# Decode kernel with attention and an MLP: most of one row set of w2 goes to other partitions, in small transfers of its own

## The chip, the core and the metric

The kernel runs on one core of one Trainium2 chip. The metric is the device time of one execution in microseconds; the time before is the median of five runs. One more execution was taken with the hardware profiler, and all views of the profile below are of that one. Times in them count from the start of its span unless a duration is meant.

## What is computed

One decoding step for two sequences: a layer norm of x, sliding-window attention over a cached K and V, and, in parallel, an MLP with a squared ReLU. Both results are added to x.

```python
B, Sq, D = 2, 1, 576;  Hq, Hkv, Sk, Dh = 32, 16, 8192, 128;  F = 4608
W = min(4096, max(256, Sk // 4))                 # 2048 keys of the window
xn = layernorm(x)
q  = (xn @ wq).reshape(B, Sq, Hq, Dh)            # k, v: the last W rows of the caches, 2 heads of q to one
p  = softmax(q @ k.T * Dh ** -0.5)
a  = (p @ v).reshape(B, Sq, Hq * Dh) @ wo
h  = relu(xn @ w1 + b1) ** 2
return x + a + (h @ w2 + b2)
```

All inputs and the output are bfloat16. Nearly all the data is read once: the windows of K and V (16.8 MB each), wq and wo (4.7 MB each), w1 and w2 (5.3 MB each).

## The kernel before

**Attention.** The window is worked in eight units u = 0 to 7, each four KV heads of one sequence. A unit's K is one load (`load_k`, L106) of 128 partitions with 16 KB each, and so is its V. `step(u)` transposes K in eight groups on TensorE (`transposes`, L264, as float32 pairs) with copies out of PSUM on ScalarE (L270) and VectorE (L272), multiplies by q (`scores`), and computes the softmax (`softmax`). The product with V of unit u - 2 (`pv`, `pv_end`) is interleaved. `pv_all` does the last two units after step 7. The sums of each head end in `ws`.

**MLP.** `mlp_h` multiplies by w1 (L366, PSUM tiles h_ps), squares (L375) into `hrow`, and turns `hrow` by 18 transposes (L380) into two PSUM tiles hp_0 and hp_1, of which eight copies (L384, ScalarE and VectorE in turn) fill `hT_sb`. hp and the scores' tiles share the PSUM tag "sc", which has two buffers. `mlp_h` stands between step 6 and step 7 in the program, and TensorE keeps the program's order (`keep_in_program_order`).

**Output.** One accumulator `out_ps` takes every product: `out_acc` does four matmuls of 144 columns, on four column strips of the array, for one row of weights per partition. First x + b2 (L422), then, after step 7 and `pv_all`, 32 rows of wo (L446), 18 rows of the first half of w2 (L448), and 18 of the second (L451). A ScalarE copy (L456) and a store (L457) end the kernel. An earlier store of the same shape (L455) goes out before them.

**w2 in memory.** w2 has 4608 rows of 576 values (1152 bytes). Row x * 2304 + 18 * p + r lies in half x on partition p as its r-th row. The first half is one load of all 18 rows (`w2a`, L438). The second is cut by rows: nine into `w2b` (L439), and six, two and one into `w2c` (L441, the list `W2P`), so that 9, 6, 2 and 1 rows land one after another.

**Queues.** SP issues all large loads in the program's order; the loads of w2 go out behind wo (L435), at the end of the program's list. ScalarE issues x, b1, b2 and the stores. The eight rows of b1 come in four transfers of two rows (L418). Completion semaphores are taken in turn from eight; a transfer waits before its issue until the one that had its semaphore last has landed.

Of the kernel before, what the change touches and what calls it, by code (L numbers as in the profile page):

```python
# [8 lines left out]
F32 = mybir.dt.float32  # L9
BF16 = mybir.dt.bfloat16  # L10
# [6 lines left out]
def kernel(  # L17
# [14 lines left out]
    nc = tc.nc  # L32
    P = 128
    B, Sq, D = A_x.shape
# [36 lines left out]
    RB = 32 * (NG4 - 1) + 2 * B  # L71
    WR = Hq * Dh // P
    WC = Dh // WR
    FR = L1 // P
    assert HW == 32 * FR and QH * 2 == NC and NC * WC == 32
    W2P = [(9, 15), (15, 17), (17, 18)]
    R9 = 9
    BS = 16
    MB = BS * (B - 1) + 1
    RM = 32 * (NG4 - 1) + MB  # L80
# [3 lines left out]
    const = ctx.enter_context(tc.tile_pool(name="const", bufs=1))  # L84
    kvpool = ctx.enter_context(tc.tile_pool(name="kvpool", bufs=6))
    wbig = ctx.enter_context(tc.tile_pool(name="wbig", bufs=1))
    w2pool = ctx.enter_context(tc.tile_pool(name="w2pool", bufs=1))
# [3 lines left out]
    psum = ctx.enter_context(tc.tile_pool(name="psum", bufs=1, space=bass.MemoryType.PSUM))  # L91

    def matmul(*a, **k):
        tc.keep_in_program_order(nc.tensor.matmul(*a, **k))  # L94

    def transpose(*a, **k):
        tc.keep_in_program_order(nc.tensor.transpose(*a, **k))  # L97
# [21 lines left out]
        nc.sync.dma_start(out=tl[:, 0:n], in_=w.rearrange("r n -> (r n)").rearrange("(p l) -> p l", p=P))  # L119
        return tl  # L120

    const.tile([P, 144], F32, name="pad_0")
    xb_sb = const.tile([B + 1, D], BF16, name="xb_sb")
    x_sb = xb_sb[0:B, :]
    nc.scalar.dma_start(out=x_sb, in_=x2d)
# [23 lines left out]
    ident = const.tile([P, P], BF16, name="ident")  # L149
# [30 lines left out]
    for t0, half, k0, n, pc in ((0, 0, 0, NK, 0), (0, 1, 0, NK, 1), (1, 0, 1, NK - 1, 1), (1, 1, 0, NK - 1, 0)):  # L180
# [11 lines left out]
                          in_=own[:].unsqueeze(2).to_broadcast([P, NC, WC]))  # L192
# [11 lines left out]
                          in_=ident[0:2 * NG4, 0:2 * NG4].rearrange("p (x g) -> p x g", g=NG4).unsqueeze(3)  # L204
# [3 lines left out]
    w2_rows = B_w2.rearrange("(x p r) n -> x p (r n)", x=2, r=FR)  # L208


    w2c_sb = w2pool.tile([P, (FR - R9) * D], BF16, name="w2c")

    out_ps = psum.tile([RM, OQ], F32, tag="out", name="out_ps")
    nc.vector.memset(out_ps[:], 0.0)
# [1 line left out]
    def out_acc(lhsT, rhs, o, start=False, stop=False):  # L216
        for i in range(4):
            matmul(out_ps[32 * i:32 * i + MB, :], lhsT=lhsT, rhs=rhs[:, o * D + i * OQ:o * D + (i + 1) * OQ],
                   start=start, stop=stop, skip_group_check=True, tile_position=(0, 32 * i))
# [38 lines left out]
    def transposes(u, g):  # L258
        k_f = k_tiles[u][:].bitcast(F32)
        kT_ps = psum.tile([P, JG * P], BF16, tag="kT", bufs=3, name=f"kT_ps_{u}_{g}")  # L260
        kT_f = kT_ps[:].bitcast(F32)
        for i in range(JG // 2):
            j = g * JG // 2 + i
            transpose(out=kT_f[:, i * P:(i + 1) * P], in_=k_f[:, j * P:(j + 1) * P], identity=ident_f[:])  # L264
        t, o = divmod(g, TG)
        if o == 0:
            kT_tiles[(u, t)] = ktpool.tile([P, TG * JG * P], BF16, tag="kT_sb", name=f"kT_{u}_{t}")
        kT = kT_tiles[(u, t)][:, o * JG * P:(o + 1) * JG * P]
        if g % 2 == 0:
            nc.scalar.copy(out=kT, in_=kT_ps[:])  # L270
        else:
            nc.vector.tensor_copy(out=kT, in_=kT_ps[:])  # L272

    def scores(u, t):
        tq, b = divmod(u, B)
        if t == 0:
            sc_tiles[u] = psum.tile([P, NJJ * 32], F32, tag="sc", bufs=2, name=f"sc_ps_{u}")
            matmul(sc_tiles[u][:], lhsT=far_h[:], rhs=is_h, start=True, stop=False, skip_group_check=True)
        sc_ps = sc_tiles[u]
        kT = kT_tiles.pop((u, t))[:].rearrange("p (j k c) -> p j k c", k=P, c=2)  # L280
        z = QZ * (1 - t)
        for c in range(2):
            for g in range(4):
                matmul(sc_ps[32 * g:32 * (g + 1), :], lhsT=qz[:, tq, b, c, z:z + SR],
                       rhs=kT[:, :, 32 * g:32 * (g + 1), c], start=False, stop=(t == NT - 1 and c == 1),
                       skip_group_check=True, tile_position=(0, 32 * g))
# [23 lines left out]
    nc.gpsimd.memset(ws[:], 0.0)  # L310
    hT_sb = const.tile([P, 2, FR, MB], BF16, name="hT_sb")
    nc.gpsimd.memset(hT_sb[:], 0.0)

    def pv(u, part, parts):
        n = NJJ // parts
        if part == 0:
            o_tiles[u] = psum.tile([P, NS * Dh], F32, tag="o", name=f"o_ps_{u}")
        v = v_tiles[u][:].rearrange("p (t j s d) -> p j t s d", t=NT, s=2, d=Dh)
        for j in range(part * n, (part + 1) * n):
            g = j % 4  # L320
            matmul(o_tiles[u][32 * g:32 * (g + 1), :], lhsT=pT_tiles[u][:, j, :], rhs=v[:, j], start=(j < 4),
                   stop=(j >= NJJ - 4), skip_group_check=True, tile_position=(0, 32 * g))
        if part == parts - 1:
            pT_tiles.pop(u)

    def pv_end(u):
        tq, b = divmod(u, B)
        o_ps = o_tiles.pop(u)
        o1 = o1_tiles.pop(u)
        for k in range(NS):  # L330
            kw = dict(out=o1[:, 0:Dh], in0=o_ps[:, k * Dh:(k + 1) * Dh])
            if k == 0:
                nc.vector.tensor_scalar(scalar1=in_s[:, 0:1], scalar2=None, op0=ALU.mult, **kw)
            else:
                nc.vector.scalar_tensor_tensor(scalar=in_s[:, k:k + 1], in1=o1[:, 0:Dh], op0=ALU.mult, op1=ALU.add,  # L335
                                               **kw)

        def fin():
            op = psum.tile([P, Dh + 1], F32, tag="op", name=f"op_ps_{u}")
            pp = slice(32 * tq, 32 * (tq + 1))  # L340
            matmul(op[pp, :], lhsT=of_h[:], rhs=o1[:], start=True, stop=True, skip_group_check=True,
                   tile_position=(0, 32 * tq))
            linv = work.tile([P, 1], F32, tag="linv", name=f"linv_{u}")
            nc.vector.reciprocal(out=linv[pp, :], in_=op[pp, Dh:Dh + 1])
            om_t = work.tile([P, Dh], F32, tag="om", name=f"om_{u}")
            om = om_t[pp, :].rearrange("p (q r) -> p q r", r=WR)
            nc.vector.scalar_tensor_tensor(out=om, in0=op[pp, 0:Dh].rearrange("p (q r) -> p q r", r=WR),
                                           scalar=linv[pp, 0:1], op0=ALU.mult, op1=ALU.mult,
                                           in1=own_c[pp, :].unsqueeze(2).to_broadcast([32, WC, WR]))
            with nc.allow_low_precision(reason="sums of one term and zeros"):  # L350
                nc.vector.tensor_reduce(out=ws[pp, :, BS * b], in_=om.rearrange("p q r -> p r q"), axis=AX.X,  # L351
                                        op=ALU.add)

        return fin

    def mlp_h(w1_sb):
# [20 lines left out]
        for a in range(2):  # L377
# [3 lines left out]
            for g in range(NG4):  # L381
# [2 lines left out]
                cp(out=hT_sb[pp, :, a * nr:(a + 1) * nr, 0:MB:BS].rearrange("p x r b -> p r x b"),  # L384
                   in_=hp[pp, :, 32 * g:32 * g + 2 * B].rearrange("p r (x b) -> p r x b", b=B))

    def step(u):
        fin = None
        w = u - 2
        with_pv = w >= 0  # L390
        for g in range(NG):
            transposes(u, g)
            if with_pv and g == 1:
                pv(w, 0, 2)
            if with_pv and g == 2:
                pv(w, 1, 2)
                fin = pv_end(w)
            if g == TG + 1:
                scores(u, 0)
            if g == TG + 2 and fin:  # L400
                fin()
        scores(u, 1)
        softmax(u)
# [10 lines left out]
    softmax(0)  # L414
    load_v(2)
    b1_rows = B_b1.rearrange("(x n) -> x n", n=HW)
    for i0, i1 in ((0, 2), (2, 4), (4, 6), (6, 8)):
        nc.scalar.dma_start(out=b1_sb[i0:i1, :], in_=b1_rows[i0:i1, :])  # L418
    nc.scalar.dma_start(out=xb_sb[B:B + 1, :], in_=B_b2.rearrange("(o n) -> o n", o=1))
    step(1)  # L420
    load_k(4)
    out_acc(sel_b[:], xb_sb, 0, start=True)  # L422
    for u in range(2, NU - 1):
        step(u)
        if u + 1 < NU - 2:
            load_v(u + 1)
        if u == 4:
            w1_sb = issue_flat(B_w1, "w1")
        if u + 3 < NU:
            load_k(u + 3)  # L430
        if u == 5:
            for v in (NU - 2, NU - 1):
                load_v(v)
    mlp_h(w1_sb)
    wo_sb = issue_flat(A_wo, "wo")  # L435
    w2a_sb = w2pool.tile([P, FR * D], BF16, name="w2a")
    w2b_sb = kvpool.tile([P, R9 * D], BF16, tag="kv", name="w2b")
    nc.sync.dma_start(out=w2a_sb[:], in_=w2_rows[0])  # L438
    nc.sync.dma_start(out=w2b_sb[:], in_=w2_rows[1, :, 0:R9 * D])  # L439
    for r0, r1 in W2P:  # L440
        nc.sync.dma_start(out=w2c_sb[:, (r0 - R9) * D:(r1 - R9) * D], in_=w2_rows[1, :, r0 * D:r1 * D])  # L441
    step(NU - 1)
    pv_all(NU - 2)
    pv_all(NU - 1)
    for r in range(WR):
        out_acc(ws[:, r, :], wo_sb, r)  # L446
    for r in range(FR):
        out_acc(hT_sb[:, 0, r, :], w2a_sb, r)  # L448
    for r in range(FR):
        w, o = (w2b_sb, r) if r < R9 else (w2c_sb, r - R9)  # L450
        out_acc(hT_sb[:, 1, r, :], w, o, stop=(r == FR - 1))  # L451

    fin_sb = work.tile([RM, OQ], BF16, tag="fin", name="fin_sb")
    out_v = out2d.rearrange("b (q n) -> q b n", q=4)
# [33 lines left out]
```

## Time and profile before

| | us |
|---|---|
| five runs, median (lowest to highest) | 134.04 (133.92 to 134.12) |
| the profiled execution | 134.12 |
| its span | 132.2 |

The profiled execution's time is 1.9 above its span, the stretch from the first to the last instruction of the trace.

| engine | busy us | share of the span | instructions |
|---|---|---|---|
| TensorE, matmuls | 84.3 | 64% | 949 |
| TensorE, weight loads | 51.8 | 39% | 949 |
| VectorE | 63.2 | 48% | 176 |
| ScalarE | 46.6 | 35% | 67 |
| GpSimd | 4.9 | 4% | 15 |

The DMA engines moved 53.76 MB at a mean of 407 GB/s. The mean granted TensorE clock was 0.815 of full speed; it was 0.50 from 82 to 103.7 and from 113.9 to 124.2, and again from 127.6 on. When the loads at the end were issued on SP, in order: wo at 95.82, w2a at 96.20, w2b at 96.68, the three of w2c between 97.15 and 101.27. The matmuls on wo start at 119.02, on w2a at 122.84, on w2b at 125.99 and on w2c at 128.09.

A row of digits in the profile has 40 equal slices; each digit is the busy share of a slice in tenths. In a row of a timeline or a chain the first two numbers are start and duration. DMA queues are listed with packets, megabytes and share of the time of 16 engines.

The trace also holds a record of each DMA packet (queue, start, duration, bytes), without the engine that moved it. A transfer ends, on each engine that takes part, with a packet of 4 bytes, the completion.

### The profile page before, as it was taken

How to read it: one execution, taken by the hardware profiler on the slowest of the kernel's cores; microseconds unless marked ns; L12 is line 12 of the kernel's file. 1: busy time of each engine (PE TensorE's matmuls, PEld its weight loads, DVE VectorE, ACT ScalarE, POOL GpSimd, SP SyncE). 2: the span in 40 equal slices, each digit the busy share in tenths (PEclk: the TensorE clock that was granted, in tenths of full speed). 3: DMA queues.
4: the chain of work that ended last, by engine and by line, in shares of the span. 5: the costliest groups of instructions: out<-in, count | busy, mean ns of one | idle time of the engine just before them, and what ended most of it. 6: DMA issues, size and time to landing. Idle time of an engine off the chain costs nothing.

```text
span 132.2 us, 2285 instructions
## 1 busy us (share of the span) xinstructions
PE 84.3 (64%) x949; PEld 51.8 (39%) x949; DVE 63.2 (48%) x176; ACT 46.6 (35%) x67; POOL 4.9 (4%) x15
## 2 busy tenths in 40 slices
PE   0079219699689779687696597003919974619651
PEld 0068102268345435353353353002418631209550
DVE  7765300325558757677496576400074477660000
ACT  5717300318846376094373563200015452000000
POOL 5000000010010010100100100100000001000000
PEclk9999975556999999999999999555555899755775
DMA  3999989999999999999999999999999999899960
GB/s 110 421 462 469 424 373 441 406 456 411 436 424 421 451 406 456 406 446 426 441 424 411 446 493 401 406 451 399 426 446 416 493 384 502 382 401 414 417 259 1
DMA packets 3511, 53.76 MB, mean 407 GB/s; under 512 B 419, under 2 KB 558, under 8 KB 814
## 3 DMA queue, kind: packets, MB, share of 16 engines
q1 hardware_dynamic: 3456, 53.61, 95.1%
q8 instruction: 7, 0.11, 0.3%
q10 hardware_dynamic: 46, 0.02, 0.0%
q14 instruction: 2, 0.02, 0.0%
HBM read 53.62 MB, written 0.00 MB: 406 GB/s over the span
## 4 chain that ended last, share of the span: by engine, by line
DMA 77%; PE 17%; SPq 2%; DVE 1%; issue 1%; ACT 0%; ACTq 0%; DVEq 0%
DMA w<-in_B_w_dram 25%; DMA w2c<-in_B_w_dram 23%; DMA k<-in_A_k_cache_dram 15%; DMA wq<-in_A_wq_dram 13%; PE kT_ps L97 6%; PE h_ps L94 3%; PE q_ps L94 3%; PE sc_ps L94 2%; PE out_ps L94 1%; PE qT_ps L97 1%; SPq L106 1%; PE o_ps L94 1%; DVE qrow L238 1%; DVE qz L254 0%; SPq L438 0%
## 5 line engine op out<-in xcount | busy, mean ns | idle before, releaser
L97 PE MATMUL kT_ps<-ident_f,k 128*128 128x128 f32 x256 | 40.2, 305 | 6.1 <-DMA k<-in_A_k_cache_dram 4.1
L97 PEld LDWEIGHTS kT_ps<-ident_f,k 128*128 128x128 f32 x256 | 31.8, 156 | 19.4 <-issue 10.7
L270 ACT COPY kT<-kT_ps 128x1024 bf16<-128x1024 bf16 x32 | 31.9, 1012 | 17.4 <-PE kT_ps L97 17.2
L272 DVE COPY kT<-kT_ps 128x1024 bf16<-128x1024 bf16 x32 | 21.8, 681 | 5.9 <-PE kT_ps L97 5.6
L94 PE MATMUL sc_ps<-kT,qz 128*32 128x512 bf16 x128 | 10.5, 413 | 6.3 <-DVE kT L272 4.7
L302 ACT ACTIVATE p<-sc_ps,bias 128x512 bf16<-128x512 f32 x8 | 5.5, 687 | 21.3 <-DVE gown L298 18.2
L94 PE MATMUL o_ps<-v,pT 128*32 128x512 bf16 x128 | 10.8, 420 | 0.0
L94 PEld LDWEIGHTS <-xnT 128*4 128x4 bf16 x108 | 3.6, 121 | 17.9 <-issue 16.3
L94 PE MATMUL h_ps<-w,xnT 128*4 128x288 bf16 x72 | 4.5, 442 | 8.7 <-DMA w<-in_B_w_dram 8.7
L305 DVE STREAM_TRANSPOSE pT<-p 128x512 bf16<-128x512 bf16 x8 | 5.7, 711 | 6.0 <-ACT p L302 6.0
L335 DVE SCALAR_TENSOR_TENSOR o<-o_ps,in_s,o 128x128 f32<-128x128 f32 x24 | 8.3, 345 | 0.4
L291 DVE TENSOR_REDUCE m<-sc_ps 128x1 f32<-128x512 f32 x8 | 5.5, 692 | 5.4 <-PE sc_ps L94 5.4
L375 DVE TENSOR_TENSOR hrow<-t 100x1152 bf16<-100x1152 f32 x2 | 2.6, 1355 | 10.4 <-ACT t L373 10.4
L94 PE MATMUL q_ps<-wq,xnT 128*4 128x512 bf16 x36 | 4.0, 627 | 5.2 <-DMA wq<-in_A_wq_dram 5.2
L295 POOL PARTITION_ALL_REDUCE gmax<-m x8 | 2.9, 367 | 105.9 <-DVE m L293 105.9
L94 PE MATMUL op_ps<-o,of_h 128*32 128x129 f32 x16 | 3.4, 299 | 4.6 <-DVE o L335 4.6
L94 PEld LDWEIGHTS <-qz 128*32 128x32 bf16 x128 | 2.2, 98 | 10.5 <-DVE kT L272 7.1
L456 ACT CAST fin_sb<-out_ps 113x144 bf16<-113x144 f32 x1 | 0.3, 280 | 17.0 <-PE out_ps L94 17.0
L97 PE MATMUL pro_ps<-ident,xn_sb 2*128 2x2 bf16 x5 | 0.9, 180 | 6.8 <-DVE xn_sb L171 6.5
L238 DVE CAST qrow<-q_ps 100x512 bf16<-100x512 f32 x1 | 0.7, 692 | 8.5 <-PE q_ps L94 8.5
L94 PE MATMUL out_ps<-wo,ws 128*17 128x144 bf16 x128 | 4.0, 325 | 1.2 <-DVE ws L351 1.2
L94 PEld LDWEIGHTS <-hT_sb 128*17 128x17 bf16 x144 | 3.5, 113 | 3.0 <-issue 2.9
(71 smaller groups left out, 58.2 us busy)
## 6 DMA issues: line engine op xcount, KB each, us to landing
k<-in_A_k_cache_dram SPq DMA_DIRECT2D x8, 2048.0 KB, 20.9
v<-in_A_v_cache_dram SPq DMA_DIRECT2D x8, 2048.0 KB, 21.1
w<-in_B_w_dram SPq DMA_DIRECT2D x1, 5184.0 KB
wq<-in_A_wq_dram SPq DMA_DIRECT2D x1, 4608.0 KB, 17.8
wo<-in_A_wo_dram SPq DMA_DIRECT2D x1, 4608.0 KB
w2a<-in_B_w_dram SPq DMA_DIRECT2D x1, 2592.0 KB, 26.6
w2b<-in_B_w_dram SPq DMA_DIRECT2D x1, 1296.0 KB
w2c<-in_B_w_dram SPq DMA_DIRECT2D x1, 864.0 KB
```

Source lines behind the costliest of these rows:

```text
L94: tc.keep_in_program_order(nc.tensor.matmul(*a, **k))
L97: tc.keep_in_program_order(nc.tensor.transpose(*a, **k))
L106: nc.sync.dma_start(out=tl[:], in_=cache[b, tq * TH:(tq + 1) * TH, S0:Sk, :].rearrange("h (c j) d -> c h (j d)", c=CP))
L238: cp(out=qrow[:, k * QW:(k + 1) * QW].rearrange("p (i a d) -> p i a d", a=2, d=Dh), in_=q_ps[0:RB, k * QW // 2:(k + 1) * QW // 2].rearrang ...
L270: nc.scalar.copy(out=kT, in_=kT_ps[:])
L272: nc.vector.tensor_copy(out=kT, in_=kT_ps[:])
L291: nc.vector.tensor_reduce(out=m1[:], in_=sc_ps[:], axis=AX.X, op=ALU.max)
L295: nc.gpsimd.partition_all_reduce(gmax[:], m2[:], channels=P, reduce_op=ReduceOp.max)
L302: nc.scalar.activation(out=p_sb[:], in_=sc_ps[:], func=ACT.Exp, bias=bias[:, 0:1], scale=scale, accum_out=o1[:, Dh:Dh + 1])
L305: nc.vector.transpose(out=pT[:].rearrange("p j r -> p (j r)"), in_=p_sb[:])
L335: nc.vector.scalar_tensor_tensor(scalar=in_s[:, k:k + 1], in1=o1[:, 0:Dh], op0=ALU.mult, op1=ALU.add, **kw)
L375: nc.vector.tensor_tensor(out=h4[:, :, k * HB:(k + 1) * HB], in0=t4, in1=t4, op=ALU.mult)
```

## The change

One row of the second half of w2, the last (r = 17), is loaded in another way; the other 17 are cut as 11, 3, 2 and 1.

Of the 128 partitions' rows r = 17, those of partitions 7, 15, 23 and so on (16 rows) go to the same partitions of a tile `w2y`, in one transfer. The other 112 go to 56 partitions of a tile `w2x`, two rows on each: partition 64 e + 32 i + 8 q + j of w2 (with j from 0 to 6) goes to partition 32 i + 4 j + q, row e. That is four transfers of 28 partitions. They are issued on SP between w2a and w2b.

The rows of h that belong to `w2x` must lie on the same partitions. `mlp_h` gets an addition at its end: ScalarE copies them out of `hrow` (`h_last`), TensorE transposes them (`hx`, a third tile of the tag "sc"), and ScalarE copies them in two pieces into `hx_sb`. The output gets two `out_acc` for `w2x` and one for `w2y`, between those of w2a and w2b: 80 matmuls for the second half instead of 72. Three memsets on GpSimd clear the new tiles, which are not filled everywhere.

The loads of b1 become seven: six of one row and one of two. `pad_0`, a tile that nobody reads, gets smaller by what the new tiles take.

```diff
-    W2P = [(9, 15), (15, 17), (17, 18)]
-    R9 = 9
+    R9 = 11
+    RL = FR - 1
+    W2P = [(R9, 14), (14, 16), (16, RL)]
+    PL = P // 2
+    NJ7 = 7
...
-    const.tile([P, 144], F32, name="pad_0")
+    const.tile([P, 88], F32, name="pad_0")
...
-    w2c_sb = w2pool.tile([P, (FR - R9) * D], BF16, name="w2c")
+    w2c_sb = w2pool.tile([P, (RL - R9) * D], BF16, name="w2c")
+    w2x_sb = w2pool.tile([PL, 2, D], BF16, name="w2x")
+    nc.gpsimd.memset(w2x_sb[:], 0.0)
+    w2y_sb = w2pool.tile([P, D], BF16, name="w2y")
+    nc.gpsimd.memset(w2y_sb[:], 0.0)
...
+    hx_sb = const.tile([PL, 2, MB], BF16, name="hx_sb")
+    nc.gpsimd.memset(hx_sb[:], 0.0)
...
+        hx = psum.tile([PL, P], BF16, tag="sc", bufs=2, name="hx")
+        h_last = const.tile([RB, PL], BF16, name="h_last")
+        nc.scalar.copy(out=h_last[:].rearrange("p (a j q) -> p a q j", a=2, j=8),
+                       in_=hrow[:, RL:PL * FR:FR].rearrange("p (a q j) -> p a q j", a=2, j=8))
+        transpose(out=hx[:, 0:RB], in_=h_last[:], identity=ident[0:RB, 0:RB])
+        for i in range(2):
+            pp = slice(32 * i, 32 * (i + 1))
+            nc.scalar.copy(out=hx_sb[pp, :, 0:MB:BS],
+                           in_=hx[pp, 0:P].rearrange("p (e i x b) -> p i x e b", e=2, i=2, b=B)[:, i, 1])
...
-    for i0, i1 in ((0, 2), (2, 4), (4, 6), (6, 8)):
+    for i0, i1 in ((0, 1), (1, 2), (2, 3), (3, 4), (4, 5), (5, 6), (6, 8)):
         nc.scalar.dma_start(out=b1_sb[i0:i1, :], in_=b1_rows[i0:i1, :])
...
     nc.sync.dma_start(out=w2a_sb[:], in_=w2_rows[0])
+    w2_last = w2_rows[1, :, RL * D:FR * D]
+    w2_move = w2_last.rearrange("(e i q j) n -> e i j q n", e=2, i=2, q=4)
+    for i in range(2):
+        for e in range(2):
+            nc.sync.dma_start(out=w2x_sb[32 * i:32 * i + 4 * NJ7, e, :], in_=w2_move[e, i, 0:NJ7])
+    nc.sync.dma_start(out=w2y_sb[NJ7:P:8, :], in_=w2_last[NJ7:P:8, :])
     nc.sync.dma_start(out=w2b_sb[:], in_=w2_rows[1, :, 0:R9 * D])
...
-    for r in range(FR):
+    for e in range(2):
+        out_acc(hx_sb[:, e, :], w2x_sb[:, e, :], 0)
+    out_acc(hT_sb[:, 1, RL, :], w2y_sb, 0)
+    for r in range(RL):
         w, o = (w2b_sb, r) if r < R9 else (w2c_sb, r - R9)
-        out_acc(hT_sb[:, 1, r, :], w, o, stop=(r == FR - 1))
+        out_acc(hT_sb[:, 1, r, :], w, o, stop=(r == RL - 1))
```

## The prediction

> **What bounds the kernel now.** I read the DMA queues first, then the chain of waits, then the end on TensorE, then the last two microseconds of DMA. All times are microseconds from the span's start.
>
> ```profile
> DMA  3999989999999999999999999999999999899960
> ...
> q1 hardware_dynamic: 3456, 53.61, 95.1%
> q8 instruction: 7, 0.11, 0.3%
> ...
> q14 instruction: 2, 0.02, 0.0%
> ```
>
> The 16 DMA engines are full from slice 2 to slice 37, and q1, the queue of SP's loads, has 95.1% of them. Time is set by when the last bytes of w2 arrive. The q8 and q14 rows are small transfers of program text that share the same engines.
>
> ```profile
> 97.15 30.90 DMA w2c<-in_B_w_dram
> 128.04 0.04 issue
> 128.09 1.36 PE out_ps L94 x34
> 129.44 0.02 issue
> 129.47 0.28 ACT fin_sb L456
> ```
>
> The chain's end is the w2c load, the matmuls on it, one copy, and the store. The instruction records refine it: w2c is three transfers (6, 2 and 1 rows). The first frees the matmuls at 128.09; they then go four per row, 0.12 a row; but the last four start at 129.12 instead of 129.00, just after SP sees the one-row transfer land at 129.09. They end at 129.42. So the end is the landing of the last row, plus 0.33, plus 0.28, plus the store.
>
> ```profile
> DMA  6899138951246544534343333354332100000000
> ...
> q1 hardware_dynamic: 198, 0.32, 38.5%
> ```
>
> This is 126.9 to 129.1 in 40 slices of 0.055. From 127.5 the busy share is 0.3 to 0.5: five to eight of 16 engines work, the rest have finished. The packet records give the completion packet of the one-row transfer on each engine: 126.89, 127.05, 127.07, 127.07, 127.14, 127.15, 127.29, 127.30; then 127.75 and 127.76; then 128.47, 128.61, 128.64, 128.66, 128.67, 128.71. Eight engines are early, two are 0.6 late, six are 1.4 late. Followed from transfer to transfer, each engine keeps its place within a few ns except for single jumps: one engine by 1.41 to 1.48 after each of the six 16 KB q8 packets before the end (at 30.1, 48.5, 67.9, 83.2, 106.6, 123.3), and one by 0.66 and one by 0.84 after the two 8 KB q14 packets. The mean of the 16 is 127.76, so perfect balance could save 0.95.
>
> **The change, part by part.**
>
> *Moved rows.* Before, row 17 of the second half is 8 packets on every engine. After, 112 of its 128 rows go in four transfers of 28, whose outer sizes are 28 and 7, and 16 rows in one transfer of 16. In the records of q10, a two-row load has two completion packets, a one-row load one, a store of 8 pieces in a 4 by 2 pattern four. So I take seven engines for each of the four transfers (4 rows each) and 16 for the fifth (1 row each): seven engines carry 17 of the rows, nine carry 1.
>
> Prices, from the first-finished engine's completions (120.62, 123.71, 125.79, 126.51, 126.89): 9 rows cost 3.093, then 6 cost 2.076, 2 cost 0.721, 1 costs 0.383. A packet is 47 ns for 1152 B and 386 for 10368 B, hence 4.6 ns plus 42.4 per row; a completion is 6 ns. After: 11 rows 8 x 471 = 3.77; 3 rows 8 x 132 = 1.06; 2 and 1 as now; the single row 0.05. Together 5.99 against 6.27. **The nine engines end 0.28 earlier; the seven 16 x 47 + 4 x 6 ns = 0.78 later than those, 0.50 later than now.** If none of the six late engines is among the seven, the last completion goes from 128.71 to 128.43. Of the seven, the early ones then end at 127.4 to 127.7 and one that is 0.6 late at 128.26.
>
> *Which seven.* The stores' packets start 6 ns after the 127.75 and 127.76 completions on two of their four engines and at once on the other two. Those four engines, to which small transfers go (I number them 0 to 3 and suppose that a transfer on seven takes 0 to 6), hold both 0.6-late engines and no 1.4-late one. For 4 to 6 I have only an order. The first late engine started its first k_0 packet among four that began together at 2.75; the other five began at 2.23, 2.33, 2.37, 2.47 and 2.48, in the order in which the text packets hit them (for the fifth the records leave 2.25 possible). Text goes round the engines in turn, it seems, and engines start in blocks. The only run of six consecutive numbers in 4 to 15 whose first has three early fellows in its block of four, and is its last, is 7 to 12. I take it, at about 8 in 10.
>
> The Trainium skill speaks against and for this. "DMA: Bandwidth & Descriptors", section "Why a DMA increments its semaphore by 16 and not by 1", has a transfer use the largest number up to 16 that divides both outer sizes, and the lowest-numbered engines: 7 for 28 and 7. Its "Rules for kernel authors" ask to use all 16 and to coalesce under 64 KB, and these move 32 KB; by its fixed 2.0 us each, five transfers in a row would add 10 and give 144. The trace agrees with the first and not the last: packets of the next transfer start 6 ns after a completion when the queue is full.
>
> *b1.* Four transfers become seven on ACT, six of one row. In the records each b1 packet waits for one wq packet of 1.36 and costs its engine 47 to 51 ns. The first engine gets 3 rows more (+0.15), the second 3 fewer (-0.15); the second is a 0.6-late one, so it ends near 128.1. Both stay below 128.43: 0 on the path. ACT issues them at 4.44 to 5.6 (1.16 for four, so +0.9), with the square root for the norm queued behind; it may also wait, as one semaphore serves every eighth transfer, until an early one lands (8.25 or 10.6). TensorE's k_0 work would begin up to 5 later, against wq at 19.17, for which the weights wait anyway. Should that cover go, unit 0 slips by 1 or 2, and the stock of four queued loads (a k load lands 20.9 after issue) hides it.
>
> *Five more issues on SP* at 96.7, 0.42 each, 2.1 in all, ahead of w2b and w2c. The queue then holds k_7, v_6, v_7, wo and w2a, some 25 of work. Semaphore reuse is the sharper edge: now the third w2c issue waits 2.9 for v_6; after, the two-row issue waits for w2a, landed at 122.7. Its packets follow 0.43 + 1.46 later (first load: issue 0.72, packet 2.19), at 124.6; early engines want them at 125.8. Cover 1.2; without it the loss is what is missing.
>
> *hx.* One copy (h_last), one transpose and two copies (about 0.3 each, as the 32x36 copies of L384) come ahead of step 7.
>
> ```profile
> 98.71 1.72 PE L97 MATMUL hp<-ident,hrow 100*128 100x100 bf16 x18 [2.94 <-DVE hrow L375]
> 100.23 1.93 PE L97 MATMUL kT_ps<-ident_f,k 128*128 128x128 f32 x8
> 102.09 1.04 PE L94 MATMUL o_ps<-v,pT 128*32 128x512 bf16 x8
> ```
>
> hx needs one of two buffers of tag sc; hp_0's last copy ends at 101.13. TensorE keeps program order, so k_7's transposes wait from 100.23 to 101.26, and pv, scores, softmax and the wo matmuls follow: +0.5 (part of this stage then runs after the granted clock rises from 0.50 to 1.00 at 103.67) to +1.03. It ends in this:
>
> ```profile
> 122.84 1.66 PE L94 MATMUL out_ps<-w2a,hT_sb 128*17 128x144 bf16 x54
> 125.71 0.48 PE L94 MATMUL out_ps<-w2a,hT_sb 128*17 128x144 bf16 x18 [1.21 <-issue]
> 125.99 0.77 PE L94 MATMUL out_ps<-w2b,hT_sb 128*17 128x144 bf16 x36
> 128.09 1.33 PE L94 MATMUL out_ps<-w2c,hT_sb 128*17 128x144 bf16 x36 [1.33 <-DMA w2c<-in_B_w_dram]
> ```
>
> The stall before 125.71 I read as waiting for the text packet of 123.3; the next wait of 1.33 is for data. The delay first eats the stall. After: 31 matmuls, then w2b's 44 once it lands at 126.7, then 12, 8, 4. At 15 ns each (as at 125.99) or 30 (as at 128.09), the first 64 of w2b and w2c need 0.96 or 1.92, and must be done by 128.84, when the last row is seen. TensorE may reach w2b as late as 126.9 at 30 ns, 127.9 at 15. Now it would be 126.2 to 126.7, with the delay half absorbed 126.5 to 127.2. I take it as hidden, thinly.
>
> *Memsets* of w2x, w2y, hx_sb on POOL: 0.3 to 0.6 each by the 0.61 one of hT_sb, early, where POOL waits 27: nothing.
>
> **Sum.** The profiled execution took 134.12 with a span of 132.2; 134.12 - 0.28 = 133.84. The last four matmuls take 0.29 now at half clock, 0.22 where the clock is full; I add -0.02. Carried to the median of 134.04, 0.08 below that execution: 134.04 - 0.30 = **133.74**; own range 133.6 to 133.9.
>
> **Rivals.** *Late engines among the seven (slower).* One of engines 4 to 6 being late now ends 0.50 later: 134.54. For it: start order alone would also allow 4 to 6. Against: the run of six. It decides as soon as one of the seven completes after 127.93 now. Chance 0.16. *TensorE takes over.* The full 1.03, no absorption, 30 ns: w2b's turn at 127.7, its 64 done at 129.6 instead of 128.84, so +0.76 - 0.28: 134.5; half of it, 134.1. Chance 0.12. *It does not do what it says*: rows spread over all 16, or the w2c issues come late and leave a gap: 134.0 to 134.3. Chance 0.06. Forecast 0.66.
>
> **Numbers.** Telling apart starts at 0.2%, 0.27: below 133.77 is faster. Of the forecast's 0.66, 0.54 lie there (several small terms, the clock above all, can only help) and 0.12 within; TensorE 0.03 within, 0.09 slower; the third 0.03 and 0.03; late engines all slower. Faster 0.54, same 0.18, slower 0.28. Range 133.55 to 134.35, which leaves out most of the first rival.
>
> **What would show it.** Six completions of the last transfer 0.28 earlier and seven 0.50 later; the low tail of DMA share shorter; the last four matmuls again released by the last row, near 128.84; k_7's transposes near 101.3. I am wrong if some engine completes after 128.7, if the last matmuls run without a wait, or if an early slice of the DMA row drops.

## The result, and the profile after

| | before | changed |
|---|---|---|
| median us (lowest to highest) | 134.07 (133.90 to 134.66, 80 runs) | 134.27 (133.71 to 135.81, 43 runs) |
| runs over 134.5 us | 5 of 80 | 13 of 43 |
| runs under 134.0 us | 14 of 80 | 5 of 43 |
| runs under 133.9 us | none | 4 of 43 |
| profiled execution, its span | 134.12, 132.2 | 133.87, 132.0 |

The ratio is 1.0019, interval [1.0011, 1.0027]: slower by about 0.2 us, where 0.3 us faster was forecast. The execution in the profile of the changed kernel is one of its few quick ones (133.87), so this profile alone misleads; usual ones, of 134.2 to 134.3, come below. First its two rows of the DMA busy share, the whole span and then 126.9 to 129.1 in slices of 0.055 us:

```profile
DMA  4999989999999999999999999999999989899970
...
q1 hardware_dynamic: 3628, 53.61, 95.4%
q8 instruction: 7, 0.11, 0.3%
```

```profile
DMA  9895796895764935526544644200000000000000
```

The queue is as full as before. q1 has 172 packets more: 128 for the row that is now loaded apart, and 44 completions, which is four transfers on seven engines and one on sixteen. The short row reaches zero six slices earlier: the last completion stands at 128.40, 0.31 before the 128.71 of the kernel before. Then TensorE's timeline in the same profile (start, duration, engine, line, tile, count, idle time before), at the start of step 7 and in the last part:

```profile
101.05 0.24 PE L100 MATMUL hx<-ident,h_last 100*64 100x100 bf16 x1 [0.73 <-ACT hT_sb L393]
101.22 1.97 PE L100 MATMUL kT_ps<-ident_f,k 128*128 128x128 f32 x8
...
124.40 1.04 PE L97 MATMUL out_ps<-w2a,hT_sb 128*17 128x144 bf16 x53
127.23 0.49 PE L97 MATMUL out_ps<-w2a,hT_sb 128*17 128x144 bf16 x19 [1.79 <-issue]
127.64 0.30 PE L97 MATMUL out_ps<-w2x,hx_sb 64*17 64x144 bf16 x8
127.87 0.24 PE L97 MATMUL out_ps<-w2y,hT_sb 128*17 128x144 bf16 x4
127.94 0.86 PE L97 MATMUL out_ps<-w2b,hT_sb 128*17 128x144 bf16 x44
128.63 0.55 PE L97 MATMUL out_ps<-w2c,hT_sb 128*17 128x144 bf16 x24
```

hx waits 0.73 for the copy out of hp_0, and k_7's transposes stand behind it. At the other end, the chain of waits closes so:

```profile
120.62 4.82 PE out_ps L97 x137
125.44 1.79 issue
127.23 1.98 PE out_ps L97 x99
```

Before, the chain ended in the load and 34 matmuls. Here 99 matmuls run without one wait for data, those of w2b at 15.7 ns each: TensorE, not the last row, sets the end of this execution, at 129.18. The semaphore of the last row was complete at 128.82 (SP, which waits for another one first, passed it at 128.91), and with 0.27 for the last four matmuls it would have allowed an end near 129.1. The two limits lie within 0.1 of each other.

### The profile page after: what moved, and what is told of

Its sections match the earlier page's. It is cut to its first block, busy times and chain, and to the rows that moved or that the text cites. A ratio compares the mean times of both kernels' runs of the same rounds, so it can differ in the third digit from the quotient of the medians.

```text
span 132.0 us, 2322 instructions
## 1 busy us (share of the span) xinstructions
PE 84.5 (64%) x958; PEld 51.0 (39%) x958; DVE 64.2 (49%) x176; ACT 47.4 (36%) x70; POOL 6.7 (5%) x18
## 4 chain that ended last, share of the span: by engine, by line
DMA 55%; PE 29%; DVE 9%; issue 3%; ACT 2%; SPq 1%; POOLq 0%; ACTq 0%; DVEq 0%
DMA w<-in_B_w_dram 25%; DMA k<-in_A_k_cache_dram 16%; DMA wq<-in_A_wq_dram 13%; PE kT_ps L100 10%; PE out_ps L97 5%; PE h_ps L97 3%; PE sc_ps L97 3%; PE q_ps L97 3%; PE o_ps L97 2%; DVE hrow L384 2%; DVE o L344 2%; PE op_ps L97 1%; PE hp L100 1%; DVE ws L360 1%; DVE om L356 1%
## 5 line engine op out<-in xcount | busy, mean ns | idle before, releaser
L100 PE MATMUL kT_ps<-ident_f,k 128*128 128x128 f32 x256 | 41.9, 311 | 8.2 <-DMA k<-in_A_k_cache_dram 6.7
L97 PE MATMUL o_ps<-v,pT 128*32 128x512 bf16 x128 | 11.4, 442 | 0.0
L97 PE MATMUL q_ps<-wq,xnT 128*4 128x512 bf16 x36 | 3.5, 559 | 4.4 <-DMA wq<-in_A_wq_dram 4.4
L342 DVE TENSOR_SCALAR o<-o_ps,in_s 128x128 f32<-128x128 f32 x8 | 2.8, 345 | 5.4 <-PE o_ps L97 5.4
L97 PEld LDWEIGHTS <-ws 128*17 128x17 bf16 x128 | 3.7, 134 | 1.6 <-issue 1.6
```

## The experiments

Three theories of the loss were written down first: A, hx waits for hp_0's buffer and makes TensorE late; B, the eight more matmuls and their place cost the time; C, the small transfers hold up other loads. All times are medians; ratios are to the kernel before on the same chip. Profile times are microseconds of the span.

### Is it the wait for hx?

`before_plus_hx` is the kernel before with h_last, hx and its copies added, not used. `no_hx` is the changed kernel without them; the products with `w2x` take rows of `hT_sb` in their place, so its output has other values:

```diff
...
-        out_acc(hx_sb[:, e, :], w2x_sb[:, e, :], 0)
+        out_acc(hT_sb[0:PL, 1, e, :], w2x_sb[:, e, :], 0)
```

`hx_late` transposes h_last after pv_all(6), in a buffer of tag kT. `hx_in_hp1` puts the transpose into the free end of hp_1's bank, from where the two copies then read:

```diff
...
-        transpose(out=hx[:, 0:RB], in_=h_last[:], identity=ident[0:RB, 0:RB])
+        transpose(out=hp_t[0:PL, nr * RB:(nr + 1) * RB], in_=h_last[:], identity=ident[0:RB, 0:RB])
...
```

> The kernel before, with h_last, the transpose of hx in a third tile of the tag sc and the two copies added; nothing reads their result. Theory A: wo's matmuls start 1.0 to 1.6 later than before and the time rises by 0.1 to 0.5, to 134.15 to 134.6, with a wider spread of runs. Theories B and C: 134.0 to 134.1, as before.

> The changed kernel without h_last, the transpose of hx and its copies; the two products with w2x take rows of hT_sb in their place, so their part of the output is of other values. Loads and matmuls as changed. Theory A: 133.65 to 133.90. Theory B: 134.2 to 134.3. Theory C: 134.2 to 134.3.

> The changed kernel, with the transpose of hx and its copies moved behind pv_all(6), into a tile of the tag kT, where TensorE waits for the softmax of unit 7. Theory A: k_7's transposes near 100.2, time 133.65 to 133.90. Theories B and C: 134.2 to 134.3.

> The changed kernel, with the transpose of hx put into the free end of hp_1's PSUM bank instead of a third tile of the tag sc; all loads and matmuls as changed. Theory A (hx waits for hp_0's buffer, TensorE reaches the end late): k_7's transposes start near 100.3 instead of 101.2, the matmuls on wo near 119.1 instead of 120.6, and the time falls to 133.65 to 133.90, below before. Theory B (eight more matmuls and their place between w2a and w2b cost the time): 134.2 to 134.3, no change. Theory C (the five small transfers hold up w2b and w2c): 134.2 to 134.3.

Measured: before_plus_hx 134.01, ratio 0.9994 [0.9980, 1.0009]; no_hx 134.24, 1.0011 [0.9998, 1.0025]; hx_late 134.27, 1.0013 [1.0000, 1.0025]; hx_in_hp1 134.13, 1.0003 [0.9989, 1.0018].

The delay exists: in before_plus_hx k_7's transposes begin at 101.22 (100.23 before) and the wo matmuls at 119.94 (119.02), and in no_hx and hx_late wo is back at 118.95 and 118.92. But the time doesn't follow it. The first kernel has the delay and loses nothing; the next two don't have it and stay at 134.25. So A doesn't carry the median. hx_in_hp1 was a bad tool: its transpose waits for the last copy out of hp_1 instead (until 102.05 in its second profile, 101.05 in the changed kernel), TensorE gets later, not earlier, and its 134.13 says nothing about A.

Why no_hx isn't at 133.75 is in its packet records. Its loads were done at 128.81, all but one engine at 128.40. That made theory D: the unequal shares take back what they bring, because a packet of program text, near 124, meets one of the seven engines that carry 17 rows and makes it late.

### Where do usual executions end?

The changed kernel and hx_late were profiled again, unchanged, and the b1 loads taken back to four:

```diff
-    for i0, i1 in ((0, 1), (1, 2), (2, 3), (3, 4), (4, 5), (5, 6), (6, 8)):
+    for i0, i1 in ((0, 2), (2, 4), (4, 6), (6, 8)):
```

> The changed kernel once more, as it is, for a profile of a usual execution (134.2 to 134.3). Theory D (the last 16 KB text packet of TensorE fell to one of the seven engines that carry 17 rows): one engine's last completion stands at 128.75 to 128.85 us of the span, 0.4 after all others, and the last four matmuls wait for it. Theory A (hx makes TensorE late): all engines are done by 128.45 and the last matmuls wait for nothing or run at 30 ns. If the execution is a quick one of 133.7 to 133.9, neither is met: last completion 128.3 to 128.45, matmuls at 15 ns.

> A second look at the changed kernel, with the same expectations as the first: by theory D an execution of 134.2 to 134.3 has its last completion at 128.75 to 128.85 us on one engine of the seven; by theory A the loads are done by 128.45 and TensorE is late or slow.

> The kernel with the hx transpose behind the last pv, looked at again, because its first profile (span 131.9) was not one of its usual spans (132.3 to 132.5). Here TensorE is not delayed by hx, so theory A allows nothing over 133.9; theory D: 134.2 to 134.3 with one engine of the seven done at 128.75 to 128.85 and the last four matmuls waiting for it; or 133.8 to 133.9 if the text packet fell to one of the nine.

> The changed kernel with the b1 loads in four transfers as before in place of seven. Theories A and D: no change, 134.2 to 134.3, as in the changed kernel. A theory that ACT's three more issues hold up what stands behind them: 133.8 to 134.0.

The single times of changed_look1, changed_look2 and hx_late_look (look1 and look2 below are the first two) were 134.19, 134.27 and 134.39. The tail of DMA share, 126.9 to 129.1, in look1:

```profile
DMA  8959769987282774526555445211101000000000
```

and in look2:

```profile
DMA  5785875797458263654445631010010010000000
```

Against the quick execution's row, which falls from 6 to 0 within four slices, there is a thin tail of ones (one engine of sixteen is 0.6 of a tenth) up to slice 31 and 33: one engine works alone. TensorE and the chain in look1:

```profile
128.18 0.36 PE L97 MATMUL out_ps<-w2c,hT_sb 128*17 128x144 bf16 x12 [0.17 <-DMA w2c<-in_B_w_dram]
128.90 0.61 PE L97 MATMUL out_ps<-w2c,hT_sb 128*17 128x144 bf16 x12 [0.36 <-DMA w2c<-in_B_w_dram]
```

```profile
123.31 5.91 DMA w2c<-in_B_w_dram
129.22 0.04 issue
129.27 0.27 PE out_ps L97 x4
```

TensorE waits for w2c again, and the last four matmuls start at 129.27, later than before's 129.12. In no_hx and hx_late_look, where hx doesn't make TensorE late (wo at 118.95 and 118.69), they start no earlier, at 129.34 and 129.40. (That the chain shows w2c from 123.31, SP's late issue, is no gap: the engines were full until 126.9.)

Last completions by the packet records, the last engine and the next one:

| profile (its own time) | last | next | engine met by the text packet near 124 |
|---|---|---|---|
| changed, quick (133.87) | 128.40 | 128.37 | one of nine |
| hx_late (134.20, span 131.9) | 128.29 | 128.26 | one of nine |
| look1 (134.19) | 128.74 | 128.46 | one of seven |
| look2 (134.27) | 128.81 | 128.39 | one of seven |
| no_hx (134.31) | 128.81 | 128.40 | one of seven |
| hx_late again (134.39) | 128.87 | 128.32 | one of seven |
| b1_as_before (135.29) | 128.80 | 128.45 | one of seven |
| hx_in_hp1 again (134.27) | 128.83 | 128.49 | one of seven |
| hx_in_hp1 (135.93) | 128.57 | 128.53 | one of nine |

The engine is inferred, not recorded. Each engine keeps its place from load to load: from its completion of wo to its last completion one of the nine needs 12.13 us, one of the seven 12.13 + 0.78, and the one that the text packet near 124 (its start at 122.9 to 125.5) meets 1.45 more. In six of the nine profiles, those of the usual executions and of b1_as_before's long one, the last completion fits 12.13 + 0.78 + 1.45 after one of wo's completions, within 14 ns; so the text met one of the seven. In the two quick spans, and in hx_in_hp1's first profile, it fits 12.13 + 1.45 within 15 ns: one of the nine. The five engines that earlier text packets had made late belong to the nine in all of these: 12.91 after their completions of wo, which came at 115.99 or later, would be 128.90 or later, and no completion stands there.

Two times in that list don't fit their loads. hx_late's first has a span of 131.9, yet 134.20, since 2.3 us lay outside the span and not 1.9 as in the others. hx_in_hp1's first took 135.93 with its loads done early: its last matmuls ran from 127.90 to 131.27 without a wait for a load, with the granted clock at 0.50 from 128.00 on.

b1_as_before came to 134.47, 1.0036 [1.0017, 1.0055], where A and D had said 134.2 to 134.3. Part of that is explained below.

> The changed kernel with the hx transpose in hp_1's bank, looked at again, since its first profile was of an execution far off its usual one. Half of its runs were quick ones of 133.9 to 134.1, half 134.1 to 134.25. Theory D: in a quick one the last completion is at 128.3 to 128.6 and the last text packet fell to one of the nine; in the others one engine of the seven is done at 128.7 to 128.85. Theory A: last completion 128.4 either way and TensorE without a late start, wo at 119.

As theory D has it: 134.27, last completion 128.83 on one of the seven. But here the last 99 matmuls run from 127.50 to 129.62 without a wait, so TensorE alone would give the same end. B and C would have fitted the times of no_hx and hx_late in size, but neither makes one engine of sixteen late.

### Taking the unequal shares away

`spread16` sends all 128 rows to `w2x`, in four transfers of 32 partitions which all engines share. `five_engines` and `four_engines` have NJ7 = 5 and 4, and three or four transfers of 16 partitions for the rest:

```diff
-    NJ7 = 7
+    NJ7 = 5
...
-    nc.sync.dma_start(out=w2y_sb[NJ7:P:8, :], in_=w2_last[NJ7:P:8, :])
+    for j in range(NJ7, 8):
+        nc.sync.dma_start(out=w2y_sb[j:P:8, :], in_=w2_last[j:P:8, :])
```

> The changed kernel with the same work on TensorE and ACT and as many rows on other partitions, but the rows go in four transfers of 32 partitions, which sixteen engines share, so that every engine carries 8 rows as in the kernel before. Theory D (usual executions of the changed kernel end late because the last text packet meets an engine that carries 17 rows): the last completion is back at 128.6 to 128.75 us whatever engine the text met, time 133.95 to 134.1, as the kernel before. Theory A (the wait for hx, TensorE late): unchanged, 134.2 to 134.3.

> The changed kernel with 80 rows in transfers of 5 by 4 partitions (five engines, 19 rows each) and 48 rows in three transfers of 16 partitions (3 rows on each engine). Theory D: if the last text packet falls to one of these five, the last completion is at about 128.9 (17 rows gave 128.74 to 128.88, two rows more at 47 ns) and the time at 134.3 to 134.4; if it falls to one of the two now left out, at about 128.5 and 133.85 to 133.95. Theory A: 134.2 to 134.3 either way, since hx is as before.

> The same with 64 rows in transfers of 4 by 4 partitions (four engines, 20 rows each) and 64 rows in four transfers of 16 partitions (4 rows on each engine). Theory D: last text packet on one of the four: last completion at about 128.95, time 134.35 to 134.45; on another engine: about 128.55 and 133.9 to 134.0. Theory A: 134.2 to 134.3.

Measured 135.63, 137.81 and 138.70: none within any theory's numbers, and none tells D from A. SP's issues in five_engines say why:

```profile
95.65 0.34 SPq L122 DMA_DIRECT2D wo<-in_A_wo_dram  x1
96.04 0.42 SPq L457 DMA_DIRECT2D w2a<-in_B_w_dram  x1
96.56 3.24 SPq L462 DMA_DIRECT2D w2x<-in_B_w_dram  x4
100.82 16.21 SPq L464 DMA_DIRECT2D w2y<-in_B_w_dram  x3
122.93 0.35 SPq L465 DMA_DIRECT2D w2b<-in_B_w_dram  x1
```

An issue waits until the transfer eight places before it has landed. Here w2b is the eighth after w2a, so it went out at 122.93, when w2a was in, and the engines ran dry (119 to 127, slices of 0.2):

```profile
DMA  9942942793279512200000009964039788495945
```

In the changed kernel w2b is the sixth after w2a and goes out at 105.67, after a wait for v_7; only the loads of w2c wait for wo and for w2a, with the queue still full. Two transfers more cost 3.5 us. In spread16 no such gap opened, but w2b's packets took 575 ns on average, where the changed kernel has 474 to 478; why is open.

Then the shares alone. `row_whole` loads the last row of all 128 partitions by one transfer in the place of the five; hx and all matmuls stay, and those of w2x meet zeros:

```diff
-    for i in range(2):
-        for e in range(2):
-            nc.sync.dma_start(out=w2x_sb[32 * i:32 * i + 4 * NJ7, e, :], in_=w2_move[e, i, 0:NJ7])
-    nc.sync.dma_start(out=w2y_sb[NJ7:P:8, :], in_=w2_last[NJ7:P:8, :])
+    nc.sync.dma_start(out=w2y_sb[:], in_=w2_last)
```

`half_moved` moves only the rows of the first 64 partitions; `half_moved_hp1` joins this with hx in hp_1's bank.

> The changed kernel with the last row of all 128 partitions loaded by one transfer of 128 partitions in the place of the five (into w2y; w2x keeps its zeros), so that every engine carries 8 of these rows; TensorE's and ACT's work, hx included, is untouched. Theory D (the last text packet meets an engine with 17 rows): last completion back at 128.6 to 128.75 us, time 133.95 to 134.1. Theory A (TensorE late through hx): as the changed kernel, 134.2 to 134.3. If five transfers in place of one cost something by themselves (theory C), also 133.95 to 134.1, but then with the changed kernel's late engine not being one of the seven, which the looks already speak against.

> Only the 56 rows of the first half of the partitions go to other partitions (two transfers of 7 by 4); the other 72 stay, in two transfers. Seven engines then carry 13 rows in place of 17, the others 4 or 5 in place of 1. Theory D: a last text packet on one of the seven gives 128.80 - 4 x 0.047 = 128.61, the late ones among the others 128.40 + 3 or 4 x 0.047 = 128.54 to 128.59: last completion 128.6 whichever it meets, time 133.9 to 134.0. Theory A: 134.2 to 134.3.

> The same with the hx transpose in the free end of hp_1's bank, so that it waits for no copy and TensorE is not delayed. Theory D: last completion 128.6, time 133.85 to 133.95, with fewer executions above it than without this. Theory A: 133.7 to 133.8. If this trick is worth nothing: as half_moved.

Measured 134.43, 135.47 and 134.75. In the two half-moved kernels w2b's packets were stretched too (510 and 516 ns), loads were done at 129.14, and TensorE was late as well (wo at 120.07 and 120.79): a failed attempt at a better kernel, which tells nothing on D. In row_whole's profile the last completion was at 128.73, as D said, and the cast began at 129.41, no later than before's 129.47. Yet its time was 134.31. The rest lay behind the cast: 3.03 us to the end of the span, against 2.76 in both kernels. SP passed five semaphore waits there after the output had landed, some 65 ns apart, where the kernel before and the changed one pass one.

The output's semaphore is one of eight, taken in turn by all transfers, and the end waits for them in a fixed order. The kernel before has 32 transfers, the changed one 40: the same place, the last in the order. row_whole has 36, b1_as_before 37 (2.96 behind the cast). So the three more b1 loads in the change are what makes five more transfers eight. Three last runs, the first two with b1 in three loads, so 32 in all, and the third the kernel before with the changed one's seven:

> row_whole with the b1 loads in three transfers in place of seven, so that the kernel has 32 transfers in all (the kernel before 32, the changed one 40, row_whole 36). Reading of row_whole: the last completion stood at 128.72 and the cast at 129.41, as theory D said, but SP then passed five semaphore waits behind the output's landing, not one, 4 x 65 ns more. With 32 transfers the stretch from cast to end is 2.75 again, not 3.03. Theory D with this: last completion 128.6 to 128.75, time 134.0 to 134.1 in most executions, some above where TensorE is late. Theory A alone: 134.2 to 134.3. If the end's waits have nothing to do with the number of transfers: 134.4 as row_whole.

> The same with the hx transpose in hp_1's bank, so that TensorE is not delayed: even shares, 32 transfers, hx without a wait. This leaves only the change's order of loads. D and A together: 133.95 to 134.1, with fewer executions above 134.2 than row_whole_32; if the small rest of the change costs something besides, 134.2.

> The kernel before with only the b1 loads of the changed one, seven in place of four, so 35 transfers in place of 32. If the output's semaphore is one of eight taken in turn and the end waits for them in a fixed order, the stretch from the cast to the end grows from 2.75 by 3 or 4 waits of 65 ns to about 3.0, time 134.25 to 134.35; if three more issues on ACT cost nothing and the end knows nothing of their number: 134.0 to 134.1.

Measured: row_whole_32 134.14, 1.0009 [0.9994, 1.0023]; row_whole_32_hp1 134.16, 1.0013 [0.9989, 1.0038]; before_b1_7 134.30, 1.0019 [1.0009, 1.0030], with 3.01 us behind the cast. The last is the price of the output's place in that order by itself; by its chain the work before it got no later:

```profile
128.01 1.35 PE out_ps L94 x36
129.36 0.02 issue
129.38 0.28 ACT fin_sb L456
```

The cast is 0.09 earlier than before's, the time 0.24 longer. row_whole_32 has equal shares, keeps hx and the eight more matmuls, and lies 0.08 above the kernel before, with no change inside the interval; the changed kernel lies 0.20 above it. The two intervals overlap, so the times alone don't show how much of the loss the shares make. Nor does this run tell D from C, since the five small transfers go with the unequal shares; that is told by the packets, since the nine engines need the 12.13 that their rows add up to and no load is held up. row_whole_32_hp1 tells nothing on A or D: its hx waits in hp_1's bank as above, wo starts at 121.08, and its last 99 matmuls run from 127.41 to 129.52 without a wait.

The profiled row_whole_32 (134.25) still waits for its last row:

```profile
129.24 0.27 PE out_ps L97 x4
129.51 0.02 issue
129.53 0.28 ACT fin_sb L481
```

With equal shares the last completion stands at 128.63 to 128.78 in six profiles (the kernel before, before_plus_hx, before_b1_7 and the three of row_whole); with unequal ones at 128.74 to 128.87 in the six profiles of the list where the text met one of the seven, on average 0.09 later. So D accounts for the missing gain, and for some 0.1 of the loss of 0.20. Where the rest comes from, TensorE's late start or something else, is not shown.

## Why the prediction was wrong

**Moved rows: priced right.** Nine engines 0.28 earlier: from its completion of wo to its last one, an engine needed 12.42 before and one of the nine needs 12.13 after. Seven 0.78 after the nine was 0.776; seven and sixteen engines per transfer are confirmed by the 44 completions.

**Which seven: the step that failed.** "Text goes round the engines in turn, it seems ... I take it, at about 8 in 10" put all six late engines outside the seven. Five are, in all nine profiles of the list above. The sixth is among the seven in six of them and outside in the other three, so the engine that a text packet meets is not even fixed for one program. What decides it is open, and so the forecast's gain holds only in the executions where the sixth falls well. The records of one execution of the kernel before could not show that: there every engine carries the same, and the text may fall where it likes.

**Its rival had the mechanism and too high a price.** "Late engines among the seven" said 134.54, taking the last engine of before (128.71) to end 0.50 later. The one that is met ended at 128.74 to 128.87. It had completed wo at 114.38 to 114.51, so with equal shares (12.42 and 1.45 after that) it would have ended at 128.25 to 128.38, ahead of the other five late ones. In the profile of the kernel before, the text had met an engine that completed wo at 114.84 and so ended last. Hence the loss is only 0.03 to 0.16 at the landing, but the gain of 0.3 is gone. Its sign to look for, "some engine completes after 128.7", is what the usual executions show. Of the five quick runs, 133.71 to 133.93, four lie in the forecast's own range, 133.6 to 133.9; the one that was profiled (133.87) had the sixth engine outside the seven.

**hx hidden thinly: half right.** The wait of hx came as worked out (k_7's transposes at 101.22, forecast 101.26). The +0.5 to +1.03 at wo was 0.35 in look1, 0.86 in look2 and 1.60 in the quick execution. Hidden it was in look1 and look2, where the last matmuls wait for data. But "the delay first eats the stall" was wrong: the stall moved along and was not shorter, 1.22, 2.09 and 1.79 in these three against 1.21. It ends 2.3 to 2.5 us after the text packet's start in all profiles with it (packet 123.30, TensorE again at 125.71; 124.78 and 127.23), and that packet begins 3.9 to 4.9 us after wo's first matmul (4.28 before, 4.16 in the quick execution). So the whole delay arrives at w2b, in the quick execution at 127.94 in place of 125.99. What comes of it then depends on the clock. The granted clock was 1.00 from 124.37 to 131.20 in the quick execution, and its 99 matmuls just made it; in b1_as_before's profile it was 0.50 from 127.08 to 130.49, and w2b's matmuls took 30 ns each:

```profile
127.03 0.77 PE L97 MATMUL out_ps<-w2a,hT_sb 128*17 128x144 bf16 x19 [2.14 <-issue]
127.73 0.42 PE L97 MATMUL out_ps<-w2x,hx_sb 64*17 64x144 bf16 x8
128.08 0.30 PE L97 MATMUL out_ps<-w2y,hT_sb 128*17 128x144 bf16 x4
128.16 1.53 PE L97 MATMUL out_ps<-w2b,hT_sb 128*17 128x144 bf16 x44
129.48 0.94 PE L97 MATMUL out_ps<-w2c,hT_sb 128*17 128x144 bf16 x24
```

No wait for a load is left, the cast begins at 130.47 and the time is 135.29. That is the rival "TensorE takes over". It may also stand behind the changed kernel's long spans (11 of 44 are 132.6 or more; 1 of 24 with hx late or left out, none of 35 of the kernel before beside those), but that is not shown: row_whole_32 has the same matmuls and the same wait and no such span in 12, and none of the changed kernel's own long executions was profiled.

**b1, SP's issues, memsets: nothing on the path** held for the kernel as it is. For b1 it held for a reason I had not seen: the count of transfers stays a multiple of eight from before. The cover for the w2c issue held, the engines being full until 126.5, and five_engines shows what stands behind it.

**It does not do what it says**: ruled out by the packets.

**No better kernel came of it.** Of the versions run none was faster than the kernel before by more than the interval.

## What to carry to other kernels

When one transfer's share is shifted from late engines to early ones, the gain stands only if what makes them late falls on the same engines every time; profile several executions before building on it, since one profile shows one throw of the dice. Look for what a load balance can't place (program text, here 0.3% of the engines' time but 1.45 us on whichever engine it meets). And count transfers: both the eighth one back and the last one's place in the closing waits are part of the price of an extra load.

## What the runs showed that I had not expected

- The end of the kernel depends on the number of its transfers modulo eight: 32 and 40 leave 2.75 us from the cast to the end, 39 2.82, 42 2.92, 37 2.96, 35 and 43 3.01, 36 3.03.
- TensorE's stall behind a page of its program lasts until 2.25 to 2.52 us after that page's packet begins, in 18 profiles. The Trainium skill, "Runtime: NRT & Kernel Launch", section "Instruction fetch mechanics", says that the sequencer fetches 16 KiB blocks on a queue of its own and that a crossing is mostly hidden. The block size agrees with the packets of 16384 bytes. Mostly hidden it isn't here: with the engines full, TensorE stood 0.8 to 2.6 us at the crossing before w2b, and the engine that brought the page was 1.45 us late for the rest of the kernel.
- After a dry queue, sixteen engines that begin w2b together take 0.9 to 1.4 us for most of their first packets and 0.47 later; engines out of step with each other do it in 0.474 from the start.
